# Weight clamp before a bit conversion replaced by a test of all weights in layer 2, with the first block's order rewritten

## The chip, the cores and the metric

The kernel runs on one core of a Trainium2 chip. The metric is the device time of one execution in microseconds (us). PE is TensorE (matmuls), PEld its weight loads, DVE is VectorE, ACT is ScalarE, POOL is GpSimd, and SP issues the DMAs.

## The reference, cut to what matters

```python
state = alpha[:, :, t, :, None] * state + k[:, :, t] (x) v[:, :, t]   # per step t of 768, 4x8 heads of 48x48
y[:, :, t] = q[:, :, t] . state
x = y as (3072 tokens, 384)
h = maximum(x @ w_in, 0);  x = (h * h) @ w_out              # layer 1, d_ff = 2048
h = x @ w_in2;  g = h * (1 / (1 + exp(-1.702 * h)));  out = g @ w_out2   # layer 2, d_ff = 2048
```

A recurrent attention with decay `alpha` feeds two dense layers. The weights reach the reference as float64 (a float32 draw times a numpy factor), and the kernel gets them as raw 64-bit words.

## The kernel before, in words

**Tiling.** The 3072 tokens are six blocks of 512. The recurrence runs in 24 half-chunks `n` (12 chunks of 64 steps, two per chunk); four of them make one block. Each dense layer takes the hidden dimension in 16 slices `j` of 128. Per block and slice, `inner` does 9 matmuls of 128x128 by 512 (weights and activations are each split into a high and a low float32r part, and three of the four products are kept, over three pieces of the inner dimension) and `outer` another 9 into three accumulators `acc0` to `acc2`. `outer` runs two slices behind `inner`, so that ACT and DVE have time to make the high part `hi` and the low part `lo` of the activations.

**Weights.** A weight tile (layer `l`, slice `j`) is 128x768 float64 words: 768 KB, loaded by `w_load` from `wpk` (line 76). Five more steps turn it into two float32r tiles: `w_abs` (ACT, line 84: absolute value of the upper word read as float32, into `wf`), `w_bits` (DVE, four instructions, lines 91, 92, 95 and 98), `w_hi` (ACT, line 104) and `w_lo` (DVE, line 110). Line 91 clamps the value between `TINY` and `HUGE`, which keeps the later shift of the exponent inside float32's range; lines 92 to 98 mask, shift and join the bits. Layer 1's 16 tiles are converted while the first block is computed. Layer 2's 16 tiles are converted during blocks 1 to 4 of layer 1 (`w_store`), sent to a DRAM buffer `home`, and fetched back late in layer 1. In layer 2 nothing is converted.

**Attention steps of a half-chunk `n`.** `load` (three DMAs), `decays` (two scans, lines 327 and 333, and a reciprocal), `ratios` (343), `swap` (ACT, 350 and 351), `carry` (DVE, 361: state `S` times decay), `measure` (ACT, 367), `scores` (PE into `Y`, 384), `state` (PE, 397), `turn` (PE into `kp`, 410) and `turned` (ACT, 415), `causal` (DVE into `M`, 419), `intra` (PE into `X`, 432), `gain` (PE, 443), `before` (ACT, 460), `leave` (ACT for n < 2, line 466; DVE later, 468), `update` (DVE, 475), then `y_turn` (PE into `tp`, 137), `x_hi` (ACT, 142) and `x_lo` (DVE, 146), which give the first layer's input.

**What sets the order.** Every engine runs its instructions in program order. In the first block that order is the string `ORDER`, a list of steps `name:number` written out in the source, carried out one by one by `first_block`; after it, loops over blocks and slices in `fast` give the order. SP issues all DMAs in order as well: a DMA whose buffer is not free holds those behind it. The staging of layer-1 tiles uses one buffer `wraw` (j a multiple of 3) and two places in the still unused `x2`.

**The fast path's verdict.** `measure` and `x_hi` collect magnitudes in `stats`; in block 1 of layer 2 `sum_up` squares and sums them into `total`, `verdict` adds them over partitions with one matmul and compares with `LIMIT`, and in block 2 every engine loads the resulting `flag` into a register. At the end a branch runs the slower, safe function `general` if the flag is 0.

Of the kernel before, what the change touches and what calls it, by code (L numbers as in the profile page):

```python
# [32 lines left out]
ORDER = """
load:0 load:1 decays:0 load:2 w_load:2 ratios:0 decays:1 measure:0 turn:0 w_load:0 scores:0 turned:0 causal:0
load:3 w_abs:2 ratios:1 intra:0 gain:0 decays:2 measure:1 w_load:1 turn:1 w_abs:0 scores:1 leave:0 load:4 update:0
swap:2 ratios:2 turned:1 y_turn:0 x_hi:0 carry:2 turn:2 causal:1 w_abs:1 x_lo:0 intra:1 measure:2 decays:3 gain:1
scores:2 leave:1 load:5 ratios:3 swap:3 state:2 turned:2 update:1 measure:3 y_turn:1 causal:2 scores:3 carry:3
x_hi:1 w_bits:1 before:2 state:3 intra:2 before:3 gain:2 causal:3 w_hi:1 w_load:4 x_lo:1 update:2 intra:3 leave:2  # L40
load:6 w_bits:0 turn:3 y_turn:2 turned:3 gain:3 x_hi:2 x_lo:2 load:7 w_hi:0 leave:3 update:3 y_turn:3 w_lo:0 x_hi:3
decays:4 w_load:3 x_lo:3 swap:4 ratios:4 inner:0 w_abs:3 w_lo:1 measure:4 w_bits:2 w_abs:4 turn:4 relu:0 scores:4
square:0 w_bits:3 inner:1 g_hi:0 w_load:5 turned:4 w_hi:2 relu:1 g_lo:0 square:1 w_load:6 g_hi:1 w_lo:2 outer:0
w_hi:3 g_lo:1 w_abs:5 w_lo:3 inner:2 w_bits:5 w_abs:6 outer:1 relu:2 square:2 carry:4 w_load:8 w_bits:4 g_hi:2
w_hi:5 state:4 inner:3 before:4 g_lo:2 w_hi:4 w_load:7 causal:4 outer:2 relu:3 w_lo:4 square:3 g_hi:3 w_lo:5
intra:4 g_lo:3 w_abs:8 gain:4 w_bits:6 w_abs:7 inner:4 load:8 outer:3 w_bits:7 relu:4 w_load:9 w_hi:6 square:4
g_hi:4 inner:5 leave:4 w_hi:7 w_load:10 g_lo:4 update:4 outer:4 relu:5 w_lo:7 square:5 w_lo:6 g_hi:5 g_lo:5 w_abs:9
y_turn:4 w_bits:8 inner:6 x_hi:4 w_abs:10 outer:5 relu:6 w_bits:9 square:6 w_load:11 w_hi:8 g_hi:6 inner:7 g_lo:6
w_hi:9 w_load:12 w_lo:8 outer:6 relu:7 w_lo:9 square:7 g_hi:7 decays:5 w_abs:11 inner:8 w_abs:12 g_lo:7 swap:5
relu:8 w_bits:10 outer:7 square:8 g_hi:8 inner:9 g_lo:8 w_load:13 w_hi:10 carry:5 x_lo:4 w_lo:10 outer:8 relu:9  # L50
square:9 w_bits:11 g_hi:9 inner:10 w_abs:13 ratios:5 w_hi:11 w_load:14 relu:10 g_lo:9 turn:5 square:10 w_lo:11
scores:5 g_hi:10 state:5 w_bits:12 turned:5 outer:9 measure:5 before:5 w_abs:14 inner:11 causal:5 w_hi:12 w_load:15
g_lo:10 w_lo:12 intra:5 relu:11 decays:6 outer:10 square:11 g_hi:11 w_abs:15 inner:12 g_lo:11 swap:6 ratios:6
carry:6 measure:6 scores:6 w_bits:13 outer:11 relu:12 square:12 g_hi:12 gain:5 decays:7 w_hi:13 state:6 load:9
before:6 leave:5 swap:7 w_lo:13 update:5 carry:7 y_turn:5 causal:6 inner:13 x_hi:5 ratios:7 x_lo:5 measure:7
w_bits:14 turn:7 scores:7 relu:13 turn:6 square:13 state:7 turned:7 turned:6 intra:6 g_lo:12 before:7 gain:6
w_hi:14 causal:7 outer:12 update:6 g_hi:13 leave:6 w_lo:14 g_lo:13 y_turn:6 intra:7 w_bits:15 x_hi:6 gain:7
inner:14 update:7 w_hi:15 outer:13 x_lo:6 relu:14 leave:7 w_lo:15 square:14 g_hi:14 decays:8 inner:15 y_turn:7
g_lo:14 relu:15 ratios:8 x_hi:7 outer:14 swap:8 square:15 x_lo:7 carry:8 measure:8 scores:8 g_hi:15 state:8 g_lo:15
turn:8 before:8 causal:8 turned:8  # L60
"""
# [734 lines left out]
```

## Time and profile before

| | |
|---|---|
| median of 3 runs (lowest to highest) | 909.18 us (908.87 to 911.0) |
| the profiled execution, its span | 912.27 us, 910.6 us |
| mean granted TensorE clock | 0.978 of full speed |
| PE busy, 6575 matmuls | 881.9 us (97%) |
| DVE busy, 842 instructions | 523.7 us (58%) |
| ACT busy, 721 instructions | 390.1 us (43%) |
| read from and written to HBM | 61.45 MB, 17.30 MB |

The profiled execution's own time is its span and 1.67 us around it. Busy time is the union of an engine's instructions; lines of the DVE overlap by some 0.08 us at their ends where one doesn't wait for the other, so the distance from start to start is what one costs. Matmuls are pipelined: a busy PE need not be at its peak.

### The profile page before, as it was taken

Reading aid. Unit: us, or ns where it says so; the run is one execution under the profiler, and the core shown is the slowest. Engines: PE = TensorE matmul, PEld = TensorE weight load, DVE = VectorE, ACT = ScalarE, POOL = GpSimd, SP = SyncE. Lnnn points to the kernel's source line nnn. Section 1 sums busy time; section 2 is a strip of 40 time slices with the busy share of each in tenths; the row PEclk is TensorE's granted clock in tenths of the full one; section 3 lists DMA queues with packets and bytes.
Section 4 is the critical chain, followed back from the end, with each engine's and each line's share of the span. In section 5 each row is a group of like instructions: output and inputs, shape, how many; then the busy total and the mean of one; then the engine's idle time right before and its main releaser. Section 6 shows DMA issues by size and latency. Waiting matters only on the chain.

```text
span 910.6 us, 15677 instructions
## 1 busy us (share of the span) xinstructions
PE 881.9 (97%) x6575; PEld 721.4 (79%) x6575; DVE 523.7 (58%) x842; ACT 390.1 (43%) x721; POOL 2.1 (0%) x12
## 2 busy tenths in 40 slices
PE   6789799999999999999999999999999999999997
PEld 4577678888888888888888888888888888888885
DVE  7999988776876877676523333333333333343332
ACT  4477655545444544544433333333333332333332
POOL 0000000000000000000000000000000000000000
PEclk7799889999999999999999999999999999999999
DMA  8554312433444333362055500000000000000001
GB/s 321 202 203 152 111 41 92 136 114 114 153 151 151 114 114 116 126 211 73 36 190 191 174 0 1 35 1 0 35 1 1 35 0 1 35 1 1 35 1 39
DMA packets 24399, 79.85 MB, mean 88 GB/s; under 512 B 2560, under 2 KB 5632, under 8 KB 24320
## 3 DMA queue, kind: packets, MB, share of 16 engines
q1 hardware_dynamic: 24320, 78.76, 25.1%
q8 instruction: 54, 0.88, 0.4%
q14 instruction: 25, 0.20, 0.1%
HBM read 61.45 MB, written 17.30 MB: 86 GB/s over the span
## 4 chain that ended last, share of the span: by engine, by line
PE 81%; DVE 11%; issue 3%; ACT 2%; DMA 2%; SPq 1%; DVEq 0%; ACTq 0%
PE acc L215 38%; PE h L174 38%; DVE wf L95 1%; DVE w L110 1%; PE kp L410 1%; DMA x<-wpk 1%; PE Y L384 1%; PE X L432 1%; DVE wf L92 1%; PE Y L397 1%; DVE lo L200 1%; DMA wraw<-wpk 1%; DVE raw L343 1%; DVE wf L98 1%; DVE wf L91 1%
## 5 line engine op out<-in xcount | busy, mean ns | idle before, releaser
L174 PE MATMUL h<-x,w 128*128 128x512 f32 x1728 | 428.7, 393 | 1.9 <-ACT x L142 0.7
L174 PEld LDWEIGHTS h<-x,w 128*128 128x128 f32 x1728 | 324.0, 189 | 71.4 <-DVE x L146 1.1
L215 PE MATMUL acc<-hi,w 128*128 128x512 f32 x1152 | 301.0, 393 | 2.0 <-ACT hi L193 2.0
L215 PEld LDWEIGHTS acc<-hi,w 128*128 128x128 f32 x1152 | 216.2, 189 | 47.3 <-ACT hi L193 2.4
L200 DVE TENSOR_TENSOR lo<-g,hi 128x512 fp32r<-128x512 f32 x192 | 132.9, 692 | 73.5 <-ACT hi L193 66.6
L163 DVE TENSOR_TENSOR g<-h,g 128x512 f32<-128x512 f32 x96 | 66.5, 693 | 180.8 <-ACT g L162 180.8
L215 PE MATMUL acc<-lo,w 128*128 128x512 f32 x576 | 167.2, 392 | 0.9 <-DVE lo L200 0.8
L162 ACT ACTIVATE g<-h 128x512 f32<-128x512 f32 x96 | 57.5, 599 | 187.7 <-PE h L174 187.4
L215 PEld LDWEIGHTS acc<-lo,w 128*128 128x128 f32 x576 | 108.6, 189 | 25.1 <-DVE lo L200 2.4
L184 ACT ACTIVATE g<-h 128x512 f32<-128x512 f32 x96 | 57.3, 597 | 144.6 <-PE h L174 132.1
L193 ACT CAST hi<-g 128x512 fp32r<-128x512 f32 x112 | 69.4, 620 | 73.2 <-DVE g L163 72.8
L193 DVE CAST hi<-g 128x512 fp32r<-128x512 f32 x80 | 34.0, 425 | 112.1 <-ACT g L189 112.1
L189 ACT ACTIVATE g<-g 128x512 f32<-128x512 f32 x96 | 60.7, 632 | 3.0
L327 DVE TENSOR_TENSOR_SCAN raw<-raw,c 128x520 f32<-128x520 f32 x20 | 24.7, 1234 | 2.1 <-DMA raw<-qka 2.1
L333 DVE TENSOR_TENSOR_SCAN raw<-raw,c 128x520 f32<-128x520 f32 x20 | 24.8, 1242 | 0.7
L367 ACT ACTIVATE raw<-raw 128x1040 f32<-128x1040 f32 x20 | 21.3, 1063 | 7.6 <-DVE raw L343 7.6
L343 DVE TENSOR_TENSOR raw<-raw 128x1024 f32<-128x1024 f32 x20 | 24.4, 1219 | 0.0
L84 ACT ACTIVATE wf<-wraw 128x768 f32<-128x768 f32 x22 | 19.7, 896 | 5.9 <-DMA wraw<-wpk 4.6
L95 DVE SCALAR_TENSOR_TENSOR wf<-wraw,wf 128x768 int32<-128x768 int32 x22 | 21.1, 958 | 0.8
L98 DVE SCALAR_TENSOR_TENSOR wf<-wraw,wf 128x768 int32<-128x768 int32 x22 | 21.1, 958 | 0.8
L432 PE MATMUL X<-v,M 64*64 64x48 f32 x768 | 18.2, 234 | 3.2 <-DVE M L419 3.2
L137 PE MATMUL tp<-ident,y 128*128 128x128 f32 x72 | 12.8, 289 | 7.9 <-DVE y L468 4.2
(80 smaller groups left out, 472.0 us busy)
## 6 DMA issues: line engine op xcount, KB each, us to landing
wraw<-wpk SPq DMA_DIRECT2D x22, 768.0 KB, 7.0
w<-home SPq DMA_DIRECT2D x16, 768.0 KB, 4.3
raw<-qka SPq DMA_DIRECT2D x20, 512.0 KB, 4.8
x<-wpk SPq DMA_DIRECT2D x10, 768.0 KB, 4.4
home<-whi SPq DMA_DIRECT2D x16, 384.0 KB, 5.8
home<-wf SPq DMA_DIRECT2D x16, 384.0 KB, 5.6
raw<-qka SPq DMA_DIRECT2D x20, 260.5 KB, 2.8
v<-vs SPq DMA_DIRECT2D x24, 192.0 KB, 4.8
```

Source lines behind the costliest of these rows:

```text
L95: nc.vector.scalar_tensor_tensor(out=fi, in0=high, scalar=-0x40000000, in1=fi, op0=ALU.bitwise_and, op1=ALU.bitwise_or,)
L98: nc.vector.scalar_tensor_tensor(out=fi, in0=low, scalar=29, in1=fi, op0=ALU.logical_shift_right, op1=ALU.bitwise_or,)
L162: nc.scalar.activation(out=g, in_=h, func=AF.Sigmoid, scale=1.702)
L163: nc.vector.tensor_tensor(out=g, in0=h, in1=g, op=ALU.mult)
L174: self.nc.tensor.matmul(h, lhsT=w[:, a, kk * 128:(kk + 1) * 128], rhs=x[:, b, kk, :], start=(i == 0), stop=(i == 3 * KK - 1),)
L184: self.nc.scalar.activation(out=g, in_=h, func=AF.Relu)
L189: self.nc.scalar.activation(out=g, in_=g, func=AF.Square)
L193: copy(hi, self.h_t[key, j][1])
L200: self.nc.vector.tensor_tensor(out=lo, in0=g, in1=hi.bitcast(F32), op=ALU.subtract)
L215: nc.tensor.matmul(acc[m], lhsT=w[:, a, DM + m * 128:DM + (m + 1) * 128], rhs=g, start=(j == 0 and p == 0), stop=(j == NJ - 1 and p == 2),)
L343: nc.vector.tensor_tensor(out=x, in0=x, in1=r, op=ALU.mult)
L432: nc.tensor.matmul(s["X"][w][to:to + 64, hp * D:(hp + 1) * D], lhsT=M[p, w, hp * CH:(hp + 1) * CH], rhs=s["v"][p, h * D:(h + 1) * D], star ...
```

## The change

Line 91 is no longer executed on the fast path (`w_bits` has a switch `clamp`, which only `general` sets). In its place the fast path tests all 32 weight tiles again during layer 2: each is loaded once more into a `raw` buffer (`test_load`), ACT takes the absolute values of the upper words and sums them per partition (`test_sum`), and DVE takes the smallest per partition (`test_least`). A tile's load is issued at an even count `u` of slices, its sum two slices later, its minimum one slice after that, from block 0, slice 4 to block 4, slice 5. `counted` compares the 32 sums with `HUGE` and the 32 minima with `LEAST` and counts the passes; `verdict` moves from block 1, slice 6 to block 4, slice 14, sums two columns with one matmul, and sets the flag if both conditions hold; the register load moves from block 2, slice 0 to block 5, slice 4. The list `ORDER` is new; it holds the same steps with the same numbers.

```diff
-load:0 load:1 decays:0 load:2 w_load:2 ratios:0 decays:1 measure:0 turn:0 w_load:0 scores:0 turned:0 causal:0
...
+load:0 load:1 decays:0 load:2 ratios:0 load:3 decays:1 scores:0 measure:0 turn:0 w_load:0 turned:0 causal:0
...
-    def w_bits(self, l, j):
+    def w_bits(self, l, j, clamp=False):
...
-        nc.vector.tensor_scalar(out=f, in0=f, scalar1=TINY, scalar2=HUGE, op0=ALU.max, op1=ALU.min)
+        if clamp:
+            nc.vector.tensor_scalar(out=f, in0=f, scalar1=TINY, scalar2=HUGE, op0=ALU.max, op1=ALU.min)
...
+    def test_load(c):
+        t = raw_p.tile([128, WIDE], F32, tag="raw", name="test")[:, 0:4 * DM]
+        nc.sync.dma_start(out=t.bitcast(I32), in_=wpk[c // NJ, c % NJ].bitcast(I32))
+        tests[c] = t
+
+    def test_sum(c):
+        f = conv_p.tile([128, 2 * DM], F32, tag="wf", name="test_f")
+        high = tests[c].rearrange("p (n two) -> p n two", two=2)[:, :, 1]
+        nc.scalar.activation(out=f, in_=high, func=AF.Abs, accum_out=ends[:, c:c + 1])
+        tests[c] = f
+
+    def test_least(c):
+        nc.vector.tensor_reduce(
+            out=ends[:, 2 * NJ + c:2 * NJ + c + 1], in_=tests.pop(c), axis=mybir.AxisListType.X, op=ALU.min)
+
+    def counted():
+        half = ends[:, 0:2 * NJ], ends[:, 2 * NJ:]
+        nc.vector.tensor_scalar(out=half[0], in0=half[0], scalar1=HUGE, scalar2=None, op0=ALU.is_lt)
+        nc.vector.tensor_scalar(out=half[1], in0=half[1], scalar1=LEAST, scalar2=None, op0=ALU.is_ge)
+        nc.vector.tensor_reduce(out=count, in_=ends, axis=mybir.AxisListType.X, op=ALU.add)
...
-        nc.tensor.matmul(fp[0:1, 0:1], lhsT=total, rhs=ones, start=True, stop=True)
-        nc.vector.tensor_scalar(out=flag, in0=fp[0:1, 0:1], scalar1=LIMIT, scalar2=None, op0=ALU.is_lt)
+        nc.tensor.matmul(fp[0:1, 0:2], lhsT=ones, rhs=totals, start=True, stop=True)
+        nc.vector.tensor_scalar(out=fit, in0=fp[0:1, 0:1], scalar1=LIMIT, scalar2=None, op0=ALU.is_lt)
+        nc.vector.tensor_scalar(
+            out=flag, in0=fp[0:1, 1:2], scalar1=128 * 4 * NJ - 0.5, scalar2=fit, op0=ALU.is_gt, op1=ALU.mult)
...
+                u = bi * NJ + j - 4
+                c = u // 2
+                if u % 2 == 0:
+                    if 0 <= c < 2 * NJ:
+                        test_load(c)
+                    if 0 <= c - 1 < 2 * NJ:
+                        test_sum(c - 1)
+                elif 0 <= c - 1 < 2 * NJ:
+                    test_least(c - 1)
+                if bi == 4 and j == 12:
+                    counted()
+                if bi == 4 and j == 14:
                     verdict()
-                if bi == 2 and j == 0:
+                if bi == 5 and j == 4:
                     fine = nc.values_load(flag[0:1, 0:1], min_val=0, max_val=1)
...
-                net.w_bits(l, j)
+                net.w_bits(l, j, clamp=True)
```

What moves in the first block is seen in the built programs. Line numbers of the two programs differ by up to 6 here (91 is gone, 92 becomes 95, 343 becomes 349, 466 becomes 472). The first place is the first weight conversion on DVE, after `carry:3`. Before:

```order
L361 TENSOR_TENSOR S1_100<-S1_100,r0_357 128x384
L91 TENSOR_SCALAR wf_289<-wf_289 128x768
L92 TENSOR_SCALAR wf_289<-wf_289 128x768
L95 SCALAR_TENSOR_TENSOR wf_289<-x2_102,wf_289 128x768
L98 SCALAR_TENSOR_TENSOR wf_289<-x2_102,wf_289 128x768
L419 TENSOR_TENSOR M_101<-Y_0_386,mask_93 128x256
```

And now:

```order
L367 TENSOR_TENSOR S1_102<-S1_102,r0_368 128x384
L95 TENSOR_SCALAR wf_256<-wf_256 128x768
L98 SCALAR_TENSOR_TENSOR wf_256<-wraw_189,wf_256 128x768
L101 SCALAR_TENSOR_TENSOR wf_256<-wraw_189,wf_256 128x768
L481 TENSOR_TENSOR S0_101<-X_1_393,S0_101 128x4x48
```

Four instructions became three, and the first tile converted is number 0 (from `wraw`) in place of number 1 (from `x2`); all 16 conversions of the first block lose the same instruction.

The second place is ACT near the start, from `measure:0` on. Before:

```order
L367 ACTIVATE raw_111,stats_96<-raw_111 128x2x520
L415 COPY raw_111<-kp_161 128x512
L84 ACTIVATE wf_193<-x2_102 128x768
L367 ACTIVATE raw_116,stats_96<-raw_116 128x2x520
L84 ACTIVATE wf_240<-wraw_166 128x768
L466 COPY y_260<-X_0_196 128x4x48
L466 COPY y_260<-X_1_197 128x4x48
```

And now:

```order
L373 ACTIVATE raw_113,stats_96<-raw_113 128x2x520
L421 COPY raw_113<-kp_184 128x512
L373 ACTIVATE raw_118,stats_96<-raw_118 128x2x520
L472 COPY y_253<-X_0_196 128x4x48
L472 COPY y_253<-X_1_197 128x4x48
L86 ACTIVATE wf_256<-wraw_189 128x768
L421 COPY raw_118<-kp_258 128x512
L356 COPY r0_271<-x2_104 64x8
L357 COPY r0_271<-x2_104 64x8
L86 ACTIVATE wf_276<-x2_104 128x768
L86 ACTIVATE wf_314<-x2_104 128x768
L373 ACTIVATE x2_104,stats_96<-x2_104 128x2x520
```

`leave:0` (466, now 472) stood behind two `w_abs` and now stands ahead of all of them; the three first `w_abs` (tiles 0, 2 and 1) now stand ahead of `measure:2` and, behind that, `leave:1`. On DVE `update:0` waits for `leave:0`, and `update:1` for `leave:1`, in both programs. On SP the loads of half-chunk 3 now stand ahead of the three first weight loads; before, two of these stood ahead of them.

The third place is DVE at the end of the first block, from `w_lo:15` to `carry:8`. Before:

```order
L110 TENSOR_TENSOR w15_1448<-wf_1149,w15_1448 128x768
L327 SCALAR_TENSOR_TENSOR raw_795<-raw_795,c1_94 128x520
L331 RECIPROCAL c2_95<-raw_795 128x8
L333 SCALAR_TENSOR_TENSOR raw_795<-raw_795,c2_95 128x520
L200 TENSOR_TENSOR lo_1485<-g_1460,hi_1466 128x512
L343 TENSOR_TENSOR raw_795<-raw_795 128x1024
L146 TENSOR_TENSOR x_879<-tp_1481,x_879 128x3x128
L361 TENSOR_TENSOR S0_99<-S0_99,r0_1500 128x384
```

And now:

```order
L113 TENSOR_TENSOR w15_1445<-wf_1122,w15_1445 128x768
L203 TENSOR_TENSOR lo_1454<-g_1416,hi_1451 128x512
L333 SCALAR_TENSOR_TENSOR raw_867<-raw_867,c1_94 128x520
L337 RECIPROCAL c2_95<-raw_867 128x8
L339 SCALAR_TENSOR_TENSOR raw_867<-raw_867,c2_95 128x520
L149 TENSOR_TENSOR x_895<-tp_1456,x_895 128x3x128
L349 TENSOR_TENSOR raw_867<-raw_867 128x1024
L367 TENSOR_TENSOR S0_101<-S0_101,r0_1486 128x384
```

The same eight instructions stand there in another order, and `carry:8` is the last of them in both. Counted from the program's start to `carry:8`, DVE's list has 194 rows before and 178 now; the 16 that are missing are line 91's.

## Rows read from the trace of the kernel before

**Rows 1.** The page: engine line (busy, share, instructions); busy tenths of 40 slices

```profile
PE 881.9 (97%) x6575; PEld 721.4 (79%) x6575; DVE 523.7 (58%) x842; ACT 390.1 (43%) x721; POOL 2.1 (0%) x12
...
PE   6789799999999999999999999999999999999997
DVE  7999988776876877676523333333333333343332
```

**Rows 2.** Busy time by stretch: length, PE, PEld, DVE, ACT, POOL (instructions), PEclk, DMA share, GB/s

```profile
20.00:120.00 100.00, 86.38 (x947) 67.15 (x947) 97.38 (x149) 64.20 (x119) 0.00 (x0) 0.86 0.45 158
95.00:100.00 5.00, 5.00 (x62) 4.08 (x53) 4.90 (x9) 4.07 (x8) 0.00 (x0) 0.66 0.38 126
140.00:500.00 360.00, 359.38 (x3402) 297.24 (x3401) 247.29 (x425) 170.77 (x335) 0.00 (x0) 1.00 0.39 132
520.00:890.00 370.00, 370.00 (x1634) 306.11 (x1633) 137.43 (x202) 123.08 (x208) 0.00 (x0) 1.00 0.03 11
```

**Rows 3.** Chain that ended last, 40 to 136 us, shares by line

```profile
by line: DVE wf L95 10.1%; DVE w L110 10.0%; DMA wraw<-wpk 7.7%; issue 7.1%; DVE wf L98 7.1%; DVE lo L200 6.6%; PE h L174 6.5%; DVE wf L92 6.0%; DVE wf L91 5.0%; PE acc L215 4.0%; DVE raw L343 2.5%; DVE raw L327 2.4%; DVE y L468 2.2%; PE kp
```

**Rows 4.** Groups on DVE, 0 to 136 us: names, shapes, count | busy us, mean ns | idle

```profile
L91 DVE TENSOR_SCALAR wf<-wf 128x768 f32<-128x768 f32 x16 | 8.9, 554 | 0.0
```

**Rows 5.** DVE in order of time: start us, length us, line, op [idle before <-releaser]

```profile
61.78 0.69 DVE L200 TENSOR_TENSOR lo<-g,hi 128x512 fp32r<-128x512 f32 x1
62.38 0.55 DVE L91 TENSOR_SCALAR wf<-wf 128x768 f32<-128x768 f32 x1
62.97 0.56 DVE L92 TENSOR_SCALAR wf<-wf 128x768 int32<-128x768 int32 x1
```

**Rows 6.** The same view, DVE and then ACT, first 24 us

```profile
18.07 0.62 DVE L475 TENSOR_TENSOR S<-X,S 128x192 f32<-128x192 f32 x2 [2.25 <-ACT y L466]
...
21.00 0.92 ACT L84 ACTIVATE wf<-x 128x768 f32<-128x768 f32 x1 [0.87 <-DMA x<-wpk]
23.05 0.54 ACT L466 COPY y<-X 128x192 f32<-128x192 f32 x2
```

**Rows 7.** The same view, DVE and then PE, 134 to 137 us

```profile
134.78 0.55 DVE L361 TENSOR_TENSOR S<-S,r 128x384 f32<-128x384 f32 x1
...
135.38 0.68 PE L397 MATMUL Y<-S,raw 48*64 48x48 f32 x32 [0.24 <-DVE S L361]
...
136.41 2.32 PE L174 MATMUL h<-x,w 128*128 128x512 f32 x9
```

**Rows 8.** The same view, PE, 37 to 151 us

```profile
37.57 2.93 PE L174 MATMUL h<-x,w 128*128 128x512 f32 x6 [0.67 <-ACT x L142]
...
93.97 0.66 PE L410 MATMUL kp<-ident,raw 128*128 128x128 f32 x4 [2.49 <-DVE raw L343]
...
95.64 2.93 PE L215 MATMUL acc<-hi,w 128*128 128x512 f32 x6
...
113.37 4.18 PE L174 MATMUL h<-x,w 128*128 128x512 f32 x9 [0.62 <-DVE S L475]
...
144.68 1.52 PE L215 MATMUL acc<-hi,w 128*128 128x512 f32 x6
...
146.72 2.20 PE L174 MATMUL h<-x,w 128*128 128x512 f32 x9
...
148.86 0.69 PE L384 MATMUL Y<-raw 48*64 48x64 f32 x32
...
150.87 1.66 PE L215 MATMUL acc<-hi,w 128*128 128x512 f32 x6
```

**Rows 9.** Group of layer 2 on DVE; Abs of weights on ACT, 0 to 136 us

```profile
L163 DVE TENSOR_TENSOR g<-h,g 128x512 f32<-128x512 f32 x92 | 63.7, 693 | 170.6 <-ACT g L162 170.6
...
L84 ACT ACTIVATE wf<-wraw 128x768 f32<-128x768 f32 x6 | 5.4, 907 | 5.9 <-DMA wraw<-wpk 4.6 <-DVE wf L92 1.3
```

**Rows 10.** Weight loads: all (count, KB, median us to landing); longest in the chain

```profile
wraw<-wpk SPq DMA_DIRECT2D x22, 768.0 KB, 7.0
...
5.33 9.40 DMA x<-wpk
```

More of the change, by code (lines that the diff above doesn't have):

```diff
@@ L31 @@
 HUGE = 122876.0
+LEAST = 1.125 * TINY
 ORDER = """
-load:0 load:1 decays:0 load:2 w_load:2 ratios:0 decays:1 measure:0 turn:0 w_load:0 scores:0 turned:0 causal:0
-load:3 w_abs:2 ratios:1 intra:0 gain:0 decays:2 measure:1 w_load:1 turn:1 w_abs:0 scores:1 leave:0 load:4 update:0
-swap:2 ratios:2 turned:1 y_turn:0 x_hi:0 carry:2 turn:2 causal:1 w_abs:1 x_lo:0 intra:1 measure:2 decays:3 gain:1
-scores:2 leave:1 load:5 ratios:3 swap:3 state:2 turned:2 update:1 measure:3 y_turn:1 causal:2 scores:3 carry:3
@@ L40 @@
[L40 to L59, printed above, removed]
@@ L60 @@
-turn:8 before:8 causal:8 turned:8
+load:0 load:1 decays:0 load:2 ratios:0 load:3 decays:1 scores:0 measure:0 turn:0 w_load:0 turned:0 causal:0
+ratios:1 w_load:2 intra:0 gain:0 decays:2 measure:1 scores:1 w_load:1 leave:0 w_abs:0 turn:1 causal:1 turned:1
+load:4 swap:2 update:0 w_abs:2 ratios:2 intra:1 gain:1 carry:2 w_abs:1 decays:3 scores:2 measure:2 load:5 state:2
+leave:1 y_turn:0 update:1 swap:3 ratios:3 x_hi:0 y_turn:1 before:2 turn:2 x_hi:1 x_lo:0 causal:2 measure:3 x_lo:1
+intra:2 carry:3 turned:2 scores:3 w_bits:0 gain:2 state:3 load:6 update:2 w_hi:0 turn:3 leave:2 before:3 causal:3
@@ new lines @@
+y_turn:2 turned:3 w_lo:0 intra:3 x_hi:2 w_load:3 w_bits:1 gain:3 load:7 x_lo:2 w_hi:1 leave:3 decays:4 y_turn:3
+w_abs:3 w_load:4 x_hi:3 x_lo:3 swap:4 ratios:4 inner:0 carry:4 measure:4 w_lo:1 update:3 w_abs:4 w_bits:2 inner:1
+relu:0 square:0 g_hi:0 w_bits:4 w_load:5 w_hi:2 turn:4 relu:1 scores:4 square:1 g_lo:0 state:4 w_load:7 turned:4
+w_lo:2 outer:0 w_hi:4 w_bits:3 g_hi:1 w_abs:5 inner:2 before:4 g_lo:1 w_load:6 w_hi:3 w_lo:4 outer:1 relu:2 w_lo:3
+square:2 w_bits:5 g_hi:2 w_abs:7 inner:3 w_abs:6 g_lo:2 w_load:8 w_hi:5 w_bits:6 outer:2 relu:3 square:3 g_hi:3
@@ new lines @@
+inner:4 w_lo:5 w_hi:6 w_load:9 g_lo:3 w_abs:8 causal:4 outer:3 w_lo:6 relu:4 square:4 w_bits:8 g_hi:4 inner:5
+w_abs:9 g_lo:4 w_hi:8 w_load:11 w_bits:7 outer:4 relu:5 square:5 g_hi:5 w_lo:8 intra:4 w_load:10 w_hi:7 gain:4
+g_lo:5 w_abs:11 inner:6 leave:4 w_lo:7 load:8 update:4 w_bits:9 y_turn:4 relu:6 outer:5 square:6 g_hi:6 x_hi:4
+g_lo:6 w_abs:10 w_load:12 inner:7 x_lo:4 w_hi:9 decays:5 outer:6 relu:7 square:7 ratios:5 g_hi:7 swap:5 inner:8
+g_lo:7 measure:5 carry:5 w_bits:10 scores:5 relu:8 outer:7 square:8 g_hi:8 w_lo:9 w_load:13 w_hi:10 g_lo:8 w_abs:12
@@ new lines @@
+inner:9 w_lo:10 w_bits:11 turn:5 relu:9 state:5 turned:5 outer:8 before:5 causal:5 w_load:14 w_abs:13 w_bits:12
+square:9 intra:5 g_hi:9 inner:10 w_hi:11 g_lo:9 w_load:15 w_hi:12 w_lo:11 outer:9 w_lo:12 relu:10 w_abs:14
+w_bits:13 square:10 g_hi:10 inner:11 w_abs:15 g_lo:10 w_hi:13 decays:6 gain:5 relu:11 outer:10 load:9 square:11
+g_hi:11 leave:5 swap:6 update:5 inner:12 carry:6 g_lo:11 ratios:6 y_turn:5 relu:12 outer:11 w_lo:13 measure:6
+w_bits:14 square:12 g_hi:12 scores:6 x_hi:5 inner:13 x_lo:5 w_hi:14 g_lo:12 decays:7 state:6 relu:13 outer:12
@@ L61 @@
+square:13 before:6 g_hi:13 causal:6 swap:7 turn:6 ratios:7 intra:6 turned:6 carry:7 gain:6 measure:7 w_lo:14 turn:7
+scores:7 update:6 state:7 leave:6 turned:7 g_lo:13 y_turn:6 before:7 inner:14 causal:7 x_hi:6 w_bits:15 intra:7
+relu:14 gain:7 square:14 x_lo:6 outer:13 w_hi:15 update:7 leave:7 g_hi:14 w_lo:15 g_lo:14 y_turn:7 inner:15
+decays:8 x_hi:7 outer:14 relu:15 x_lo:7 swap:8 ratios:8 square:15 g_hi:15 carry:8 scores:8 measure:8 g_lo:15 turn:8
+state:8 turned:8 causal:8 before:8
 """
@@ L288, in fast @@
     stats = const.tile([128, 2 * NHS], F32, name="stats")
-    total = const.tile([128, 1], F32, name="total")
+    totals = const.tile([128, 2], F32, name="totals")
+    total, count = totals[:, 0:1], totals[:, 1:2]
+    ends = const.tile([128, 4 * NJ], F32, name="ends")
+    fit = const.tile([1, 1], F32, name="fit")
     flag = const.tile([1, 1], I32, name="flag")
@@ L480, in sum_up @@
         nc.scalar.activation(out=stats, in_=stats, func=AF.Square, accum_out=total)
+    tests = {}
+    def test_load(c):
[15 more added lines that the diff above has]
+        nc.vector.tensor_reduce(out=count, in_=ends, axis=mybir.AxisListType.X, op=ALU.add)
     def verdict():
         fp = ps.tile([128, 512], F32, tag="ps", name="fp")
-        nc.tensor.matmul(fp[0:1, 0:1], lhsT=total, rhs=ones, start=True, stop=True)
-        nc.vector.tensor_scalar(out=flag, in0=fp[0:1, 0:1], scalar1=LIMIT, scalar2=None, op0=ALU.is_lt)
+        nc.tensor.matmul(fp[0:1, 0:2], lhsT=ones, rhs=totals, start=True, stop=True)
+        nc.vector.tensor_scalar(out=fit, in0=fp[0:1, 0:1], scalar1=LIMIT, scalar2=None, op0=ALU.is_lt)
+        nc.vector.tensor_scalar(
+            out=flag, in0=fp[0:1, 1:2], scalar1=128 * 4 * NJ - 0.5, scalar2=fit, op0=ALU.is_gt, op1=ALU.mult)
     idle = net.xpool.tile([128, 640], BF16, tag="x", name="idle")
@@ L625, in fast @@
                     sum_up()
-                if bi == 1 and j == 6:
+                u = bi * NJ + j - 4
[10 more added lines that the diff above has]
+                if bi == 4 and j == 14:
                     verdict()
-                if bi == 2 and j == 0:
+                if bi == 5 and j == 4:
                     fine = nc.values_load(flag[0:1, 0:1], min_val=0, max_val=1)
```

## Prediction

> **What bounds the kernel now.** I read the page's engine line first, then its slices [rows 1]: PE is busy for 97% of the span, DVE for 58%, so PE seems to be the limit. The slices say where that is not so. In the first six, some 140 us, PE reads 6 to 9 and DVE reads 9 nearly throughout; later PE stands at 9 and DVE at 2 to 7. The stretches give the two regimes in numbers [rows 2]: from 20 to 120 us DVE is busy 97.38 of 100 us, PE 86.38 at a mean granted clock of 0.86; from 140 to 500 us PE is busy 359.38 of 360 us at full clock, and in layer 2, from 520 to 890 us, 370.00 of 370. From about 140 us on only matmuls set the time, and anything on DVE or ACT has to be late before it counts. In the first block the chain of waits runs mostly through DVE [rows 3]: the weight conversion alone (lines 91, 92, 95, 98 and 110) holds 38% of 40 to 136 us, line 91 alone 5.0%.
>
> Where the first block ends matters too. `carry:8` on DVE (134.78 us) releases `state:8` on PE at 135.38, and PE's next group but one, block 1's first `inner` at 136.41, begins the stretch without gaps [rows 7]. So the end moves with `carry:8`, as long as PE has by then done all that stands ahead of it.
>
> **The sum.** It is made against the profiled execution, 912.27 us; the median of the runs, 909.18, lies 3.09 us lower, and I shift by that at the end.
>
> *The clamp in the first block.* There are 16 of line 91 before 136 us, mean 554 ns [rows 4]. The distance that one takes out of DVE's line is from its start to the next one's start, 62.97 - 62.38 = 0.59 us [rows 5]: the next instruction needs its result, so nothing overlaps. The first instruction of a conversion then simply starts where line 91 did. 16 x 0.59 = **-9.4 us** on DVE ahead of `carry:8`. The order's third place shows that nothing else was added to or taken from DVE's list up to there.
>
> *The clamp in layer 2's conversions.* Another 16 lie in blocks 1 to 4 of layer 1, in the stretch where PE is never idle and DVE is busy 247.29 of 360 us [rows 2]. The cover is PE's matmuls: 0. Without that cover it would be worth 9.4 us again.
>
> *The start.* DVE stood idle for 2.25 us before `update:0`, which waited for ACT's `leave:0` [rows 6]; that stood behind two weight `w_abs`. The new order puts `leave:0` ahead of them, so this wait goes. What is late next is `update:1`: it waits for `leave:1`, and that now stands behind three `w_abs`, of which the last needs the third weight tile. In the old trace the third tile landed at 21.00 us and `leave:1` started at 23.05 [rows 6]; the same loads stand ahead of it now (four half-chunks and three tiles), so I expect the same 23 to 24 us. DVE would be ready for `update:1` at about 21.4 (my estimate: idle from 18.07 - 2.25 = 15.8 in the old trace, then 5.6 us of `causal:1`, `update:0`, `ratios:2`, `carry:2` and `decays:3`) and would wait some 2.2 us: the stall moves by 5 us and keeps its size. I take 0; the ends are -2.2 (tile 1 lands earlier) and +1 (ACT is later still).
>
> *The first block's PE.* From the first `inner` to `state:8` PE has 16 `inner` and 15 `outer`, 2.04 us each (144.68 to 146.72), up to 2.14 beside other shapes (146.72 to 148.86), and per half-chunk four attention groups of 2.01 us together (148.86 to 150.87), `kp` with 0.66 and `tp` with about as little [rows 8]. That is 31 x 2.09 = 65 us plus four half-chunks at 3.1, some 12: 77 us. The first groups run at half clock: six matmuls take 2.93 us at 37.57, where six at full clock take 1.52 [rows 8]; I count 4 us for that. The old order left 135.4 - 37.6 = 97.8 us for these 81, so PE lost 17 us more. I leave the first `inner` at 37.6: `x_hi:3`, which it needs, now stands on ACT behind `w_abs:3`, whose tile can be loaded only when conversion 0 has freed its buffer, and that eats the two clamps ahead of it. With `carry:8` 9.4 us earlier, 88.4 us are left and 7.4 may be lost. PE still follows DVE, but a late h will now make DVE wait more often. No row shows how often. Two of the old losses were waits for DVE itself with half clock behind them: 2.49 us at 93.97 for line 343 and 2.93 - 1.52 = 1.4 after it, 0.62 us at 113.37 for line 475 and 4.18 - 2.14 = 2.0 after it [rows 8], 6.5 us in all. The lower end is 0, if the other 10.5 shrink to 7.4 as well; the upper is +3.1, if only these two go. I take +1, nearer to the lower end: what makes PE wait is mostly DVE, and DVE gets quicker.
>
> *The tests in layer 2.* 32 loads of 768 KB, 32 sums on ACT, 32 minima on DVE, five small instructions. An `Abs` of this size takes 907 ns on ACT [rows 9]. No row shows a minimum; per element it lies between line 91's 554 ns for 768 [rows 4] and line 163's 693 ns for 512, which gives 1.04 us for 768 [rows 9]; I take 1.04, the one-element-a-step row being the nearer in kind. A slice lasts 370 us / (1634 / 18) = 4.08 us [rows 2]. Every second slice ACT gets 0.9 us more and is busy 123.08 of 370 us now; DVE gets 1.0 us more and is busy 137.43 of 370. Behind the sum wait the next slice's sigmoid, and behind that PE two slices on; behind the minimum, the next `g`. Per slice that is 1.36 us of ACT and 1.52 of DVE now, so either has over 2.5 us free where it needs one: 0, at most +1. The Trainium skill speaks against this part: by "VectorE: DVE Perf Modes", The perf-mode tier table, a float32 `tensor_scalar` in SBUF moves two elements per cycle and a `tensor_reduce` one, so the change swaps quick instructions for as many slow ones; lines 91 and 163 agree on the two rates. By that rule DVE as a whole gains work; what it would make of the time stands among the rivals.
>
> *SP.* The test loads stand on the same queue as the output stores, each of which waits for its block's last copy. A test tile is loaded when its buffer comes free, four slices (16.3 us) before its sum; 7.0 us is the median landing of such a load, 9.4 us the longest in the chain, at the crowded start [rows 10]. DMA is busy 3% of layer 2 [rows 2]. 0.
>
> The verdict's later place is hidden like the old one. Sum: -9.4 + 0 + 1 + 0 = **-8.4 us**, so 903.9 us for a profiled execution like the old one, and 909.18 - 8.4 = **900.8 us** for the median.
>
> **Rivals.**
> - *PE takes over in the first block.* More of PE's old losses stay than the 7.4 us that fit, 11 to 14, or stalls like the one at 93.97 come anew: 2.49 us idle, then half clock (granted clock 0.66 from 95 to 100 us [rows 2], six matmuls in 2.93 us [rows 8]), about 4 us each. Gain 3 to 6: 903 to 906, about 904.5. For: PE needs 81 of 88.4 us. Against: its two longest waits were for DVE.
> - *The start's stall vanishes and DVE's waits fall too:* -12 or more, 896 to 897. Against: the third tile still comes behind the same bytes.
> - *No change* (within 2.7 us, the 0.3% that a measurement of this kernel can tell): the new list brings 7 us or more of new DVE idle time; 909. Against: DVE's list is the same work.
> - *Slower: the test loads arrive late.* Place: ACT, in layer 2. A sum there waits for its tile, and sigmoid and PE stand behind it. Two buffers, each of which needs a load, a sum (0.9) and an issue (0.5) within four slices: it decides from a landing time of 14.9 us on. At 17 us each of 16 rounds loses 2.1 us, less some 5 us of lead once: +29, 938 us. Against: 7.0 and 9.4 us [rows 10].
> - *Slower: DVE's sum of work decides.* 32 x 1.04 - 32 x 0.59 = +14.4 us, 923.6. It decides only if DVE fills two slices of layer 2, 8.16 us; it has 2 x 137.43 x 4.08 / 370 = 3.0 us in them now, and 4.1 then. Against it: [rows 2]. By the Trainium skill's rule above the case would be this one; with the formula for one element per cycle in "VectorE: DVE Perf Modes", The TRN2 errata, (768 + 151) cycles at 0.96 GHz, a minimum would be an estimated 0.96 us.
> - *The change doesn't do what it says:* if the test failed, `general` would run after the fast path and the time would be a different one altogether. With the reference's seeded weights, worked out, a partition's largest sum is 907.5 against a limit of 122876 and the smallest upper word 0.178 against 0.000034. Under 1%.
>
> **How the numbers follow.** Forecast (gain 6 to 12): 0.70. PE takes over (3 to 6): 0.14. More than 12: 0.04. Together faster by over 0.3%: 0.88. No change: 0.07. Slower: 0.05 (late loads 0.03, DVE's sum 0.01, the rest 0.01). The range of 897 to 905 us holds the forecast with its bounds (-2.2 at the start, +1 there, +3.1 at PE) and most of the first rival; it leaves out its end, no change, and the two slower cases.
>
> **What would show it.** Right: no line 91 in the first block, `carry:8` at about 127 us in place of 134.78, block 1's first `inner` close behind it, an idle time of DVE before the second `update` in place of the first, PE without gaps from 130 us on, and slices of 4.08 us in layer 2 as before. Wrong: DVE under 95% busy from 20 to 110 us with waits for ACT's `hi` (PE took over); waits of ACT for the test tiles, or slices over 4.08 us in layer 2 (the tests cost); an end of the first block at the old time.

## The result and the profile after

| | before | after |
|---|---|---|
| median (lowest to highest, runs) | 909.75 us (908.87 to 911.0, 4) | 899.81 us (899.68 to 900.29, 4) |
| the profiled execution, its span | 912.27 us, 910.6 us | 899.76 us, 898.1 us |
| mean granted TensorE clock | 0.978 | 0.986 |
| read from HBM | 61.45 MB | 86.62 MB |

The changed kernel takes 0.9891 of the old time, 95% interval [0.9874, 0.9908]: 9.9 us less where 8.4 were forecast, and 899.8 in place of the predicted 900.8. One thing about sizes first: the old kernel's profiled execution, 912.27 us, was the longest of the 17 runs of it that stand beside the first experiments (median 910.54), while the new one's is at its median. Differences between these two profiles are therefore some 2 us too large, and the terms below are sized from medians, or from profiles that lie at them.

The page of the changed kernel: engine line and slices as in [rows 1], the two groups that the tests add, and their loads.

```profile
PE 874.0 (97%) x6575; PEld 717.7 (80%) x6575; DVE 534.2 (59%) x846; ACT 418.5 (47%) x785; POOL 2.1 (0%) x12
...
PE   6799999999999999999999999999999999999996
...
DVE  7999978677776876875332344454444544443332
...
L503 DVE TENSOR_REDUCE ends<-test_f 128x1 f32<-128x768 f32 x32 | 30.3, 946 | 0.0
L499 ACT ACTIVATE test_f<-test 128x768 f32<-128x768 f32 x32 | 28.9, 903 | 0.0
...
test<-wpk SPq DMA_DIRECT2D x32, 768.0 KB, 4.4
```

Each slice is 22.5 us. PE's row reads 9 from the third slice on, where slices three to five read 8, 9 and 7 before, and DVE's falls to 7 in the sixth, where it read 8: the stretch in which DVE decides has become shorter. DVE has more work than before (534.2 us against 523.7), and the time is shorter: busy time moved from a stretch where DVE decides to one where it doesn't. A minimum takes 946 ns; 1.04 us was assumed, and the estimate of 0.96 us by the Trainium skill's formula for a float32 `tensor_tensor` (VectorE: DVE Perf Modes, The TRN2 errata) was nearer.

The stretches, columns as in [rows 2]; layer 2 is the last.

```profile
20.00:120.00 100.00, 89.18 (x1023) 70.18 (x1022) 96.03 (x150) 70.39 (x133) 0.00 (x0) 0.93 0.48 165
95.00:100.00 5.00, 5.00 (x25) 4.08 (x25) 4.93 (x10) 2.75 (x7) 0.00 (x0) 1.00 0.59 199
140.00:500.00 360.00, 360.00 (x3290) 298.78 (x3289) 231.64 (x398) 166.88 (x324) 0.00 (x0) 1.00 0.41 139
510.00:880.00 370.00, 370.00 (x1635) 306.19 (x1634) 165.72 (x239) 151.86 (x272) 0.00 (x0) 1.00 0.22 75
```

Layer 2 has 370.00 us of PE in 370 as before, 1635 matmuls or 90.8 slices of 18, 4.07 us each, with 28 us more on DVE and on ACT: the tests are hidden there. From 95 to 100 us the granted clock is 1.00 where it was 0.66 [rows 2]. From 140 to 500 us PE has no idle time left, 0.62 us before.

The first 24 us, ACT and then DVE, as in [rows 6].

```profile
20.29 0.89 ACT L86 ACTIVATE wf<-x 128x768 f32<-128x768 f32 x1 [0.98 <-DMA x<-wpk]
...
22.13 0.53 ACT L472 COPY y<-X 128x192 f32<-128x192 f32 x2
...
22.74 0.62 DVE L481 TENSOR_TENSOR S<-X,S 128x192 f32<-128x192 f32 x2 [2.31 <-ACT y L472]
```

The stall of 2.25 us is not gone. It stands before the second `update` (481) and is 2.31 us, behind `leave:1` on ACT, which stands behind the `w_abs` of the third weight tile: as forecast, place and size.

The end of the first block, DVE and then PE, as in [rows 7].

```profile
121.30 1.22 DVE L349 TENSOR_TENSOR raw<-raw 128x1024 f32<-128x1024 f32 x1
122.43 0.55 DVE L367 TENSOR_TENSOR S<-S,r 128x384 f32<-128x384 f32 x1
...
122.61 0.69 PE L390 MATMUL Y<-raw 48*64 48x64 f32 x32 [0.53 <-issue]
123.24 0.66 PE L416 MATMUL kp<-ident,raw 128*128 128x128 f32 x4
123.83 0.68 PE L403 MATMUL Y<-S,raw 48*64 48x48 f32 x32
124.44 2.37 PE L177 MATMUL h<-x,w 128*128 128x512 f32 x9
```

`carry:8` moved from 134.78 to 122.43 us, and block 1's first `inner` follows 2.0 us behind it (1.6 before). It no longer releases PE, though: `state:8` (403) starts 0.85 us after `carry:8` has ended, since the new list puts `turn:8` (416) ahead of it. PE's last wait is 0.53 us before `scores:8` (390), which reads what `ratios:8` (349) writes and starts 0.09 us after its end; the view names no releaser ("issue"). So the end still follows DVE, one instruction ahead of `carry:8`.

### The profile page after: what moved, and what is told of

It reads as the page before. It is cut to its first block, busy times and chain, and to the rows that moved or that the text cites. A ratio compares the mean times of both kernels' runs of the same rounds, so it can differ in the third digit from the quotient of the medians.

```text
span 898.1 us, 15794 instructions
## 1 busy us (share of the span) xinstructions
PE 874.0 (97%) x6575; PEld 717.7 (80%) x6575; DVE 534.2 (59%) x846; ACT 418.5 (47%) x785; POOL 2.1 (0%) x12
## 3 DMA queue, kind: packets, MB, share of 16 engines
HBM read 86.62 MB, written 17.30 MB: 116 GB/s over the span
## 4 chain that ended last, share of the span: by engine, by line
PE 87%; DVE 8%; DMA 2%; issue 2%; ACT 0%; SPq 0%; DVEq 0%; ACTq 0%
PE acc L218 41%; PE h L177 41%; DVE wf L98 2%; DMA x<-wpk 1%; DVE w L113 1%; PE Y L390 1%; PE X L438 1%; PE Y L403 1%; DVE wf L101 1%; PE X L449 1%; DVE wf L95 1%; PE kp L416 1%; PE tp L140 1%; DVE lo L203 1%; DMA x<-qka 1%
## 5 line engine op out<-in xcount | busy, mean ns | idle before, releaser
L503 DVE TENSOR_REDUCE ends<-test_f 128x1 f32<-128x768 f32 x32 | 30.3, 946 | 0.0
L499 ACT ACTIVATE test_f<-test 128x768 f32<-128x768 f32 x32 | 28.9, 903 | 0.0
L101 DVE SCALAR_TENSOR_TENSOR wf<-wraw,wf 128x768 int32<-128x768 int32 x22 | 21.1, 958 | 0.8
```

Source lines behind the costliest of these rows:

```text
L101: nc.vector.scalar_tensor_tensor(out=fi, in0=low, scalar=29, in1=fi, op0=ALU.logical_shift_right, op1=ALU.bitwise_or,)
L499: nc.scalar.activation(out=f, in_=high, func=AF.Abs, accum_out=ends[:, c:c + 1])
L503: nc.vector.tensor_reduce(out=ends[:, 2 * NJ + c:2 * NJ + c + 1], in_=tests.pop(c), axis=mybir.AxisListType.X, op=ALU.min)
```

## The experiments

**The parts alone.** The first two kernels do one half of the change each, the third drops only the tests. The first and the third leave out any look at the weights' range. Before alongside: 910.54 us (17 runs).

No clamp, old order, no tests:

```diff
-    def w_bits(self, l, j):
+    def w_bits(self, l, j, clamp=False):
...
-        nc.vector.tensor_scalar(out=f, in0=f, scalar1=TINY, scalar2=HUGE, op0=ALU.max, op1=ALU.min)
+        if clamp:
+            nc.vector.tensor_scalar(out=f, in0=f, scalar1=TINY, scalar2=HUGE, op0=ALU.max, op1=ALU.min)
...
```

> The kernel before with its old order, line 91 left out on the fast path and nothing in its place (the range of the weights is then not guarded at all, and layer 2 has no tests). Theory A (DVE's line of work sets the first block's end): 16 x 0.59 us fall out ahead of carry:8, so carry:8 comes at 134.8 - 9.4 = 125.4 us and the time falls by 9.4 us against the kernel before, whatever the order. Rival B (the new order is needed to use the time): in the old order the waits grow where the clamp was, and the gain is about half, 4 to 6 us. Rival C (PE takes over): DVE shows new waits for ACT's hi between 45 and 120 us, and the gain stays under 6 us.

The kernel before with the new list in `ORDER`, clamp kept:

> The kernel before with the clamp, but with the new order of the first block. Theory A: the order by itself gives only what it takes out of DVE's idle time: 0.96 us at the second half-chunk's scan and up to 1.7 us of later waits, so 1 to 2.7 us, and carry:8 at 132 to 134 us. Rival B: the order gives half of the change, 4 to 6 us. A third possibility: an order that fits a DVE without the clamp is no better than the old one with it: 0.

The first with the new list as well, so the change without its tests (verdict and register load stand where they stood before):

> New order, no clamp, verdict and flag as before, none of the 32 tests in layer 2 (the range of the weights is not guarded). Theory A (the tests are hidden behind PE): the changed kernel's time, 899.8 us, within 0.5 us. Rival (the tests cost through DVE or ACT work): 30.3 us of minima and 28.9 us of sums are gone, and the time falls by 3 us or more.

| | median | ratio to before, 95% | `carry:8` |
|---|---|---|---|
| old order, no clamp | 902.59 us | 0.9909 [0.9894, 0.9924] | 127.27 us |
| new order, clamp | 910.38 us | 0.9998 [0.9988, 1.0008] | 132.47 us |
| new order, no clamp, no tests | 899.22 us | 0.9878 [0.9861, 0.9894] | 122.69 us |
| the change | 899.81 us | 0.9891 [0.9874, 0.9908] | 122.43 us |

The new order alone is worth nothing that these runs can tell; the clamp alone is worth 8.0 us in the old order and 11.2 in the new. So the order earns its 3.4 us only once the clamp is gone. DVE's last copy tells where the 11.2 lie, in the new order with the clamp and then without:

```profile
902.85 0.42 DVE L237 COPY x<-acc 128x256 f32<-128x256 f32 x1 [0.39 <-ACT x L236]
```

```profile
891.68 0.42 DVE L238 COPY x<-acc 128x256 f32<-128x256 f32 x1 [0.39 <-ACT x L237]
```

Up to `carry:8` the clampless one is 132.47 - 122.69 = 9.8 us ahead, at the last copy 11.2: layer 2's clamps, which run between the two places, have the other 1.4. Where the 3.4 us went in the old order, its DVE waits show (the clampless kernel in the old order, 25 to 127 us: who waited for what, us in total, times, longest):

```profile
DVE lo L201 <- ACT hi L194: 2.2, 3, 1.1
DVE M L420 <- ACT y L461: 1.5, 1, 1.5
DVE w L111 <- ACT w L105: 0.7, 2, 0.5
```

That is 4.4 us. The kernel before, in the same stretch up to its own `carry:8`:

```profile
DVE M L419 <- ACT y L460: 1.2, 1, 1.2
DVE lo L200 <- ACT hi L193: 0.5, 2, 0.3
```

So 2.7 us of the clamps' 9.4 came back as waits of DVE for ACT. The two longest for `hi`, 1.09 and 0.85 us at 46.5 and 49.5 us, follow a stretch in which ACT itself stood 5.04 us before a weight tile landed (3.68 us in the kernel before, where DVE has its clamps to do as well):

```profile
41.92 0.92 ACT L84 ACTIVATE wf<-wraw 128x768 f32<-128x768 f32 x1 [5.04 <-DMA wraw<-wpk]
```

The changed kernel has no such wait of DVE at all between 25 us and `carry:8`. PE's first `inner` and its `state:8` in this clampless kernel, and then the first `inner` in the changed one:

```profile
35.51 4.58 PE L175 MATMUL h<-x,w 128*128 128x512 f32 x9 [0.67 <-ACT x L143]
...
127.87 0.68 PE L398 MATMUL Y<-S,raw 48*64 48x48 f32 x32 [0.19 <-DVE S L362]
```

```profile
36.86 5.79 PE L177 MATMUL h<-x,w 128*128 128x512 f32 x18 [1.00 <-ACT x L145]
```

From the first `inner` to `state:8` are 92.4 us and 87.0.

**The clamp back in layer 2's conversions alone.**

```diff
-                    net.w_bits(1, t)
+                    net.w_bits(1, t, clamp=True)
```

> The changed kernel with line 91 put back in the 16 conversions of layer 2's weights, which run in blocks 1 to 4 of layer 1. Theory A (that half of the removal was hidden behind PE): 899.8 us, no change within 0.5 us. Rival (each clamp counts wherever it stands): 16 x 0.59 us more, 909.2 us.

901.43 us (901.22 to 901.79, 5 runs), ratio 0.9901 [0.9888, 0.9915]: 1.6 us above the change. The 16 clamps under PE's matmuls were not free. PE's waits of 145 to 450 us in this kernel name the place:

```profile
PE tp L140 <- DVE y L474: 0.5, 3, 0.2
```

The kernel before has four of 0.6 us in total between 140 and 505 us, this one too, the changed one none. They are idle times; what one costs is seen from start to start, here at block 2's first turn in the changed kernel and then in this one:

```profile
218.65 2.21 PE L177 MATMUL h<-x,w 128*128 128x512 f32 x9
220.70 0.49 PE L140 MATMUL tp<-ident,y 128*128 128x128 f32 x3
```

```profile
219.06 2.20 PE L177 MATMUL h<-x,w 128*128 128x512 f32 x9
221.41 0.52 PE L140 MATMUL tp<-ident,y 128*128 128x128 f32 x3 [0.15 <-DVE y L474]
```

From `inner` to `tp` are 2.35 us in place of 2.05, so the wait of 0.15 us costs 0.3. The first `tp` of blocks 1 to 4 is 0.40, 0.71, 1.06 and 1.38 us later than in the changed kernel, with `carry:8` 0.13 later, and at most 0.04 us is added between these places: one late `y` per block makes 1.3 of the 1.6 us. So three of a block's four clamps are covered, and the one ahead of `y` is not.

**How far DVE covers the tests.** Each minimum is taken four times, and later three times.

```diff
-        nc.vector.tensor_reduce(
-            out=ends[:, 2 * NJ + c:2 * NJ + c + 1], in_=tests.pop(c), axis=mybir.AxisListType.X, op=ALU.min)
+        f = tests.pop(c)
+        for _ in range(4):
+            nc.vector.tensor_reduce(
+                out=ends[:, 2 * NJ + c:2 * NJ + c + 1], in_=f, axis=mybir.AxisListType.X, op=ALU.min)
```

> The changed kernel with every minimum taken four times in a row (the result is the same). Theory A (DVE's work in layer 2 is hidden as long as two slices, 8.16 us, hold it): DVE gets 3 x 0.95 us more in two slices, 4.0 + 2.8 = 6.8 us, and the time stays within 0.5 us. Rival (DVE's sum of work decides): 96 x 0.95 = 91 us slower. Between them: single waits of PE for lo, a few us.

920.9 us (920.1 to 921.36, 4 runs), ratio 1.0114 [1.0094, 1.0134]: neither theory. One pair of slices on DVE, in order of time:

```profile
609.23 3.91 DVE L505 TENSOR_REDUCE ends<-test_f 128x1 f32<-128x768 f32 x4
613.06 0.68 DVE L166 TENSOR_TENSOR g<-h,g 128x512 f32<-128x512 f32 x1
614.42 0.69 DVE L203 TENSOR_TENSOR lo<-g,hi 128x512 fp32r<-128x512 f32 x1 [0.69 <-ACT hi L196]
615.81 0.69 DVE L166 TENSOR_TENSOR g<-h,g 128x512 f32<-128x512 f32 x1 [0.69 <-ACT g L165]
617.19 0.69 DVE L203 TENSOR_TENSOR lo<-g,hi 128x512 fp32r<-128x512 f32 x1 [0.69 <-ACT hi L196]
617.80 0.68 DVE L154 TENSOR_TENSOR x<-x,x 128x512 fp32r<-128x512 f32 x1
618.40 1.93 DVE L505 TENSOR_REDUCE ends<-test_f 128x1 f32<-128x768 f32 x2
```

and what PE waited for in layer 2 (520 to 780 us):

```profile
PE acc L218 <- ACT hi L196: 12.8, 12, 2.1
```

This pair of slices takes 618.40 - 609.23 = 9.17 us in place of 8.16: DVE has become the longer chain, and PE waits for `hi`. By busy time DVE had room, 7.1 us of 9.17. But from the first `g` (166) to the end of the split of the next block's input (154), at 613.06 to 618.40, it needs 5.3 us for some 3.2 us of work, since `g`, `hi` and `lo` go between DVE and ACT, 0.69 us of idle time a step. What is free is 8.16 - 5.3 = 2.8 us, about three minima of 0.95 us. Line 154 stands in three of a block's eight pairs; the next pair, without it, takes 8.56 us (618.40 to the next minimum at 626.96), so such a pair has 3.4 us free. Three minima are the next run:

> The changed kernel, but each of the 32 minima in layer 2 is taken three times (64 more of 0.95 us). With four of each, a pair of slices in layer 2 took 9.16 us in place of 8.16 and the whole 21 us more. Theory A (the cover ends sharply: up to some point a minimum costs nothing, behind it each costs its whole 0.95 us of DVE): a pair takes 9.16 - 0.95 = 8.21 us or its usual 8.16, so 0 to 1.5 us are added to the changed kernel's 899.8: 899.8 to 901.3. Theory B (every added minimum costs the same share, 21 us / 96 = 0.22 us): 64 x 0.22 = +14, 913.8 us, with waits of PE for hi in every second slice.

899.94 us (899.53 to 900.42, 4 runs), ratio 0.9886 [0.9865, 0.9907], so 64 minima more cost nothing (+0.1 us), and theory A holds. Layer 2 in this kernel:

```profile
520.00:880.00 360.00, 360.00 (x1591) 297.76 (x1590) 220.67 (x298) 146.22 (x267) 0.00 (x0) 1.00 0.22 77
```

DVE has 220.67 us of work in 360 and PE no gap.

**Where the tests' 0.6 us are.** The kernel without tests is 0.6 us quicker by the medians, though layer 2's slices are the same and the two ratios' intervals overlap. Four runs look for it. First each tile's sum right behind its load in program order:

```diff
-                    if 0 <= c - 1 < 2 * NJ:
-                        test_sum(c - 1)
-                elif 0 <= c - 1 < 2 * NJ:
-                    test_least(c - 1)
+                        test_sum(c)
+                elif 0 <= c < 2 * NJ:
+                    test_least(c)
```

> The changed kernel, but each test's sum stands on ACT right behind its load's issue, in the same slice, and its minimum one slice after, so ACT waits in every second slice for a load that has just been issued (landing 4.4 us). Theory A (PE has two slices of lead): ACT's waits of up to 4 us appear, sigmoid comes late, but hi and lo still come before PE needs them: under 2 us slower. Rival (late loads reach PE, as the prediction's slower case had it): the h of every second slice is late, 32 x 1 to 2 us, 30 us or more slower.

899.43 us (899.01 to 899.75, 4 runs), ratio 0.9881 [0.9861, 0.9900], so nothing for the worse. ACT's waits of 510 to 880 us in this kernel:

```profile
ACT test_f L499 <- DMA test<-wpk: 5.4, 4, 1.5
```

Four waits and not 32: the edit didn't make the loads late. Here as in the changed kernel a load goes out when an earlier sum frees its buffer (a sum at 605.45 us, the next load's issue at 606.47) and has nearly two pairs of slices until its own sum. It is late only where an output store stands ahead of it. PE waited for none of the four. What a really late load would cost this run doesn't show.

The next two runs move the register load alone: to block 5 in the kernel without tests, and to block 2 in the changed one, there with a constant 1.

```diff
-                if bi == 2 and j == 0:
+                if bi == 5 and j == 4:
```

> New order, no clamp and no tests, but the register load stands late, in block 5, as in the changed kernel (the kernel without tests had it in block 2). What takes the 0.6 us between the two? From the end of DVE's last copy to the end of the span the changed kernel has 6.2 us and the one without tests 5.3. Theory A (the late register load holds the end back): 6.2 us there, median 899.9. Theory B (it is the tests' loads or instructions, or chance, since the kernel with the sum right behind its load has 5.34 us there with tests and a late register load): 5.3 us, median 899.2.

```diff
-                if bi == 5 and j == 4:
-                    fine = nc.values_load(flag[0:1, 0:1], min_val=0, max_val=1)
+                if bi == 2 and j == 0:
+                    fine = nc.values_load(always[0:1, 0:1], min_val=0, max_val=1)
```

> The changed kernel with all its tests, but every engine loads a constant 1 into its register in block 2 of layer 2 and not the flag in block 5, so the result of the tests decides nothing (the branch to the general path never follows them). Theory A (the late register load holds the end back): 5.3 us from DVE's last copy to the span's end, median 899.2. Theory B (tests or chance): 6.2 us, or either, and a median between 899.2 and 899.9. In both, the block of layer 2 that lasts 0.37 us longer is the one with the load.

899.52 us (898.86 to 899.98, 4 runs; ratio 0.9881 [0.9860, 0.9902]) with 5.4 us from DVE's last copy to the span's end, and 899.96 us (899.7 to 901.13, 5 runs; 0.9891 [0.9873, 0.9909]) with 6.2: the register load is not it, theory A fell in both. What goes with it is in the DMA queues. The last copy and the instruction queue in the span's last 8 us (packets, MB, share), of the changed kernel:

```profile
891.48 0.42 DVE L240 COPY x<-acc 128x256 f32<-128x256 f32 x1 [0.39 <-ACT x L239]
...
q14 instruction: 7, 0.06, 2.5%
```

and with the sum right behind its load:

```profile
891.94 0.42 DVE L240 COPY x<-acc 128x256 f32<-128x256 f32 x1 [0.39 <-ACT x L239]
...
q14 instruction: 6, 0.05, 2.0%
```

The first ends at 898.1, 6.2 us behind that copy, the second at 897.7, 5.3 us behind it. In all 14 profiles of this study, six packets go with 5.3 to 5.5 us and seven with 6.2 to 7.1. The count follows the program: over the whole execution this queue has 25 packets without tests, 26 with the sum right behind its load, 27 or 28 in the others. The output stores don't explain the end: in the changed kernel's last 2.5 us no packet of theirs moves, one of this queue does. That a seventh fetch of instructions makes the end longer is argued from this, not shown by an experiment.

**What the moved stall is worth.** `leave:1` is put ahead of the two `w_abs` that it stood behind. Nothing else moves; the list is cut here to the steps around them, and the source wraps its lines elsewhere:

```diff
...
-load:4 swap:2 update:0 w_abs:2 ratios:2 intra:1 gain:1 carry:2 w_abs:1 decays:3 scores:2 measure:2 load:5 state:2
-leave:1 y_turn:0
+load:4 swap:2 update:0 ratios:2 intra:1 gain:1 carry:2 decays:3 scores:2 measure:2
+load:5 state:2 leave:1 w_abs:2 w_abs:1 y_turn:0
...
```

> The changed kernel with one place of the new order altered: w_abs:2 and w_abs:1 stand behind leave:1 in place of ahead of measure:2. Theory A (DVE's line of work sets the first block's end, and the 2.31 us before the second update are a part of it): that wait goes, carry:8 comes 2 us earlier, at about 120.4, and the time falls by 1.5 to 2.3 us, to some 898. Rival (PE is the bound by now, or another wait takes its place): carry:8 at 122 and 899.8 us.

898.24 us (897.57 to 899.58, 4 runs), ratio 0.9873 [0.9852, 0.9893], 1.6 us below the change. `leave:1` on ACT (475) and the second `update` on DVE (484) in this kernel:

```profile
18.29 0.52 ACT L475 COPY y<-X 128x192 f32<-128x192 f32 x2
...
20.34 0.59 DVE L484 TENSOR_TENSOR S<-X,S 128x192 f32<-128x192 f32 x2
```

The wait is gone (20.34 in place of 22.74) and `carry:8` comes at 120.20. Next `w_abs:3` is also put behind `x_hi:3`:

> As the kernel with leave:1 first, and also w_abs:3 behind x_hi:3 on ACT, so that the first inner doesn't wait for the fourth weight tile. Theory A (DVE sets the end): no more than the kernel with leave:1 first, within 0.5 us, since the first inner is not what DVE waits for. Rival (PE's start counts): the first inner comes 1 us or more earlier and the time falls by as much.

898.42 us (897.84 to 899.82, 4 runs), ratio 0.9868 [0.9848, 0.9888]: no gain on top. The edit didn't bring PE's first `inner` forward (36.17 us, 34.75 with `leave:1` first): on ACT `x_hi:3` no longer stands behind a weight, but now waits 1.19 us for PE's `tp`. Last, the two edits that looked best together:

> The changed kernel with leave:1 of the first block ahead of two weight conversions' first step, and in layer 2 each tile's sum right behind its load. The first edit alone gave 898.24 us and the second alone 899.43, against 899.81 for the changed kernel. Theory A (the second edit shortens the end: the kernel with it had 5.34 us from DVE's last copy to the span's end, the ones with the sums two slices later 6.2 or more): 5.3 us there, median 897.4 to 897.8, faster than every other kernel. Theory B (the end of that one run was chance): 6.2 us there, or either, median about 898.2. In both, carry:8 as with the first edit, at 120.2 us where the loads at the start land as early as in that run, up to 121.6 where they don't.

897.17 us (896.81 to 897.45, 4 runs), ratio 0.9853 [0.9837, 0.9870]: the end is 5.3 us again, and this is the quickest kernel, 2.6 us below the change. The end of 5.3 us in the earlier run was thus not chance: both profiles with the sum right behind its load have it, and none of the seven others with tests. Why the sum's place shortens the program's end is open.

## Why the prediction was right, step by step

- **The first block's clamps, -9.4.** From the new order with the clamp to the same without clamp and tests the time falls by 11.2 us (910.38 to 899.22). `carry:8` and block 1's first `inner` move by 9.8 of them, 0.61 us per clamp. The price of 0.59 us from start to start was the right one. What the step had wrong is the releaser: in the new order PE waits for `ratios:8`, not for `carry:8`. They stand next to each other on DVE, so the sum didn't suffer.
- **Layer 2's clamps, 0.** Mis-sized: 1.6 us by the medians, 1.3 to 1.4 by the rows. "The cover is PE's matmuls" took a DVE that is late by a clamp as harmless; once a block the turn to `tp` waits at once for `y` on DVE, and 0.62 us of idle PE stood in [rows 2] to be seen.
- **The start, 0.** Right: the stall moved by 4.7 us and kept its size. The list could have removed it, as `leave:1` first shows, for 1.6 us more.
- **PE behind DVE, +1 (0 to +3.1).** In the new order 0 is what was measured. From the first `inner` to `state:8`, by the prediction's 81 us of work, PE loses 6.0 us in the changed kernel (36.86 to 123.83) and 11.4 in the clampless one with the old order (35.51 to 127.87), against 17 before. So in the old order the loss is that of the rival "PE takes over" (11 to 14), and DVE's waits for `hi` are its sign; but the gain there is 8.0 us, not the rival's 3 to 6. The rival was near, and what kept it out of the changed kernel is the order, which the prediction had treated for its start only.
- **The tests, 0 (to +1).** Right for layer 2. The free time was read from sums as over 2.5 us per slice and engine; on DVE it is 2.8 to 3.4 us per *two* slices, and one minimum of 0.95 us fits in there. The +0.6 us of the medians lies at the program's end, which no step had.
- **Late loads, DVE's sum of work.** Neither came: in the changed kernel ACT never waits for a test tile, and 96 minima in place of 32 add 0.1 us. The longest landing of a test load there is 7.0 us, and the first rival was to begin at 14.9. The Trainium skill's rule on `tensor_reduce` (VectorE: DVE Perf Modes, The perf-mode tier table) agrees with the 946 ns; it tells what an instruction costs, not whether the place has room.
- **Net.** The medians' steps, -0.2 for the order alone, -11.2 for the clamps and +0.6 for the tests, make -10.7 before rounding, against the median of 910.54 beside these runs; -9.9 was measured against the four beside the changed kernel. The forecast of -8.4 had +1 for PE that did not come and 0 for layer 2's clamps that were worth 1.6. That 900.8 us lies only 1.0 from the measured 899.8 is in part luck: the median that it started from, 909.18 of three runs, is 1.4 below that of 17.
- **What would show it.** No clamp in the first block, `carry:8` with block 1 close behind, the stall before the second `update`, PE without gaps: all came, but for what releases PE at the end of the block. `carry:8` was expected at 127 us and came at 122.43; the profile that I read was a long execution, and in the kernel with the new order and the clamp, whose median is the old kernel's, it is at 132.47 us, from which 16 x 0.59 lead to 123.0.

## What to carry to other kernels

Price an instruction by the distance to the next start, and ask of each place whether that engine decides there; 32 slow minima in a covered stretch are cheaper than 16 quick clamps in an uncovered one. Free time under another engine's work is not the length less the busy sum: take off every round trip to a second engine that stands in the loop. When an instruction leaves the critical engine, the order that was tuned with it may let part of the gain go; try the order again then, since alone it may show nothing.
